# Six small loads of the start, issued by ScalarE instead of GpSimd

## The chip, the cores and the metric

The kernel runs on one core of one Trainium2 chip. The metric is the device time of one execution in microseconds (us); lower is better. Before the change three runs gave 370.06, 370.79 and 371.65 us, a median of 370.79 us.

## What is computed

For 8 batches of 8 heads, 576 tokens and a head dimension of 64, a linear attention is computed with a learned feature map, and then a layer norm and a two-layer feed-forward network with a residual are applied to its result:

```
phi(x) = concat(exp(p - m), exp(-(p - m))),  p = x @ w_phi,  m = max|p| over the 128 features
num = phi(q) @ (phi(k)^T v);  den = phi(q) . sum_s phi(k);  a = num / (den + 1e-6)
x = a with the heads side by side: [8, 576, 512]
out = x + relu(layernorm(x) * g_ln @ w_ch1) @ w_ch2      (512 -> 2048 -> 512)
```

## The kernel before, in words

The work is cut into 32 units of two heads. A unit's 576 tokens make four full tiles of 128 for each head (the main part) and a rest of 64 tokens for each head (the tail). Tails are loaded for four units at a time, one load for each head half: 64 partitions, 4 heads, 64 floats, which is 64 KB in 256 pieces of 256 B. Main parts of the first units are loaded one unit at a time, 256 KB each for q, k and v.

A unit goes through these steps. TensorE transposes k and q (L698 for the main part, L706 for the tail, which needs the tails of both q and k). ScalarE or VectorE copies the result out of PSUM into `qkT` (L715, L713). TensorE multiplies `qkT` with `wbk` (L885 and L900, L813 and L814 for tails). VectorE takes maxima (L953, L817), ScalarE the exponentials (L967, L1033, L830), GpSimd scales v into `vv` (L977 for the main part, L986 for the tail in `vx`). TensorE then forms the products with v (L1059, L1065) and the numerators (L1125, L1133). Eight units make a pair of batches, and the feed-forward of a pair (L1389 for the first layer, L1458 for the second) runs on TensorE between the attention steps of the next.

`wbk` is the bf16 form of `w_phi`, which is needed on partitions 0 to 63 and once more on partitions 64 to 127. So `w_phi` is loaded twice into `wphi_f` (L415 and L416), and VectorE casts the two halves one after the other (L463).

The order on every engine is written ahead of time by a planner (class `Order`). Each step has a rank, a set of engines and an assumed duration; the planner runs through them, gives each a start, and the instructions are emitted in order of these starts. A few operations that come first in the program, the two loads of `w_phi` and the two first q tails (L429) among them, are emitted before the planner runs; the planner only counts time for them. The planner's steps of the start, on the two queues that matter, are these:

```
add("POOL", 1.3, -9.0, None)
add("ACT", 1.3, -9.0, None)
dma("POOL", -8.9, 65536, None, w=[("qx0", 0)], us=0.65, row=4096)
add("POOL", 0.7, -8.8, None)
dma("POOL", -8.7, 65536, None, w=[("qx1", 0)], us=0.65, row=4096)
load_main("q", 0, 1, -4.0, "ACT")
load_tails("v", 0, -3.0, "POOL")
load_main("v", 0, 1, -3.0, "ACT")
add("ACT", 1.3, -1.0,
    lambda: nc.scalar.preload_act_table_set("natural_log_exp_and_others"))
```

A load issued by ScalarE counts 0.53 us in the plan. DMAs issued by SyncE (SP) and ScalarE share eight semaphores, which they take in turn; a ninth DMA can be issued only when the one eight before it has landed. DMAs issued by GpSimd have eight of their own.

Until 75 us of the plan the planner puts small matmuls that nobody reads (L1665, writing `n_bank` from a tile of zeros) into every gap of TensorE, so that it has work. They stand in TensorE's queue like any other instruction and are always executed.

Of the kernel before, what the change touches and what calls it, by code (L numbers as in the profile page):

```python
# [359 lines left out]
def kernel(  # L360
# [13 lines left out]
    nc = tc.nc  # L374
    P = 128

    B, H, S, D = q.shape
# [35 lines left out]

    wphi_f = consts.tile([P, F], FP32, name="wphi_f")
    nc.scalar.dma_start(out=wphi_f[0:D, :], in_=w_phi)  # L415
    nc.gpsimd.dma_start(out=wphi_f[D : 2 * D, :], in_=w_phi)  # L416
    gln_sb = consts.tile([P, KC], FP32, name="gln")
    ngln = consts.tile([P, KC], FP32, name="ngln")

# [1 line left out]
    qx_bufs = [consts.tile([P, TG, 2, D], FP32, name=f"qx{i}") for i in range(2)]  # L421

    def first_q_tail(half):

        src = bass.AP(
            tensor=q.tensor, offset=q.offset + (half * S + 4 * P) * D,
            ap=[[D, 64], [2 * S * D, TG], [1, D]],
        )
        nc.gpsimd.dma_start(out=qx_bufs[0][half * 64 : half * 64 + 64, :, 0, :], in_=src)  # L429

    first_q_tail(0)
    make_identity(nc, ident)
    first_q_tail(1)

    wz = consts.tile([P, P], BF16, name="wz")
# [29 lines left out]
    for i in range(2):  # L465
# [7 lines left out]
        out=nident, in0=ident, scalar1=minus, scalar2=None, op0=ALU.mult  # L473
# [64 lines left out]
    def dma(queue, rank, nbytes, emit, r=(), w=(), us=0.53, tiles=0, row=1024, late=1.7):  # L538


        key = ("dma", len(sched.ops))
        kind = "DMA_w" if queue == "POOL" else "DMA"
        if tiles:
            packets, ns, lag = tiles * 8 + BARRIER / 0.018, 0.018, LAND_T + sched.slack[2]
            us = Turn(1.3)
        elif queue == "POOL":
            packets, ns, lag = nbytes / row / 16, 0.081, LAND_W
            if row == 4096:
                packets, ns, lag = 16 * packets, 0.022, LAND_W + late
        else:  # L550
            packets, ns, lag = nbytes / row / 16, 0.018 if row <= 256 else 0.048, LAND
            lag += sched.slack[1]
            us = 0.66 if row == 256 else us
        ns *= sched.slack[3]
        pieces = max(1, round(packets * ns / 1.2))
        lanes = ("SW", 1) if queue == "POOL" else ("HW", 1)
        add(queue, us, rank, emit, r=r, w=(key, *w), acquire=lanes, load=(kind, packets * ns))
        for i in range(pieces):
            last = i == pieces - 1
            add(kind, Move(packets / pieces, ns), rank, None, r=(key, *r) if last else (key,),  # L560
                w=(*w, key) if last else (key,), lag=lag if last else 0.0,
                release=lanes if last else None)

    def issue(queue, rank, dst, src, keys, nbytes, row=1024, hold=False, n=1):
        eng = {"SP": nc.sync, "ACT": nc.scalar, "POOL": nc.gpsimd}[queue]

        def emit():
            load = eng.dma_start(out=dst, in_=src)
            if hold:
                wait_for_w2(load)  # L570

        dma(
            queue, rank, nbytes, emit, r=[("w2 came", HOLD)] if hold else (), w=keys, row=row,
            us=0.65 if queue == "POOL" else 0.53, late=1.7 + 1.4 * (n == 0),
        )
# [5 lines left out]
    def wait_for_w2(load):  # L581
        tc.add_manual_dep(
            load.ins, w2_loads[HOLD].ins.name,
            mybir.DependencyInfo(mybir.DependencyClass.Sync, mybir.DependencyReason.DATA),
            reason="weights first",
        )

    def load_main(key, n, nu, rank, queue):

        t = {"q": q, "k": k, "v": v}[key]  # L590
        pair, i = divmod(n, H)
        g, u0 = divmod(n, HG)
        buf = v_bufs[g % NBUF] if key == "v" else qk_bufs[g % NBUF][:, "qk".index(key)]
        dst = buf[:, u0 : u0 + nu, :]
        us = range(u0, u0 + nu)
        b, h, _ = heads(pair, i, 0)
        src = bass.AP(
            tensor=t.tensor, offset=t.offset + (b * H + h) * S * D,
            ap=[[4 * D, P], [S * D, 2 * nu], [1, 4 * D]],
        )  # L600
        issue(
            queue, rank, dst.rearrange("p u (a f) -> p (u a) f", a=2), src,
            [(key + str(half), g % NBUF, u) for u in us for half in range(2)]
            + [("came", key, n)],
            262144 * nu, hold=12 <= n < 2 * H,
        )

    def load_tails(key, n, rank, queue):

        t = {"q": q, "k": k, "v": v}[key]  # L610
        pair, i = divmod(n, H)
        j = n // TG % 2
        for half in range(2):
            b, h, step = heads(pair, i, half)
            ps_ = slice(half * 64, half * 64 + 64)
            dst = vx_bufs[j][ps_, :, half, 0:D] if key == "v" else (
                qx_bufs[j][ps_, :, "qk".index(key), :]
            )
            src = bass.AP(
                tensor=t.tensor, offset=t.offset + ((b * H + h) * S + 4 * P) * D,  # L620
                ap=[[D, 64], [step * S * D, TG], [1, D]],
            )
            issue(
                queue, rank, dst, src, [(key + "x" + str(half), j)], 16384 * TG,
                row=4096 if queue == "POOL" else 256, hold=12 <= n < 2 * H, n=n,
            )
# [957 lines left out]
    for n in range(NU + 2):  # L1584
# [48 lines left out]
        if n >= 1 and n <= NU:  # L1633
# [4 lines left out]
            half, i = i % 4 // 2 if i % 2 else None, i % 4 + 4 * (i == 7)  # L1638
# [67 lines left out]
```

## Time and profile before

| what | value |
|---|---|
| three runs | 370.06, 370.79, 371.65 us |
| median | 370.79 us |
| profiled execution, its own time | 369.84 us |
| its span, first to last instruction | 367.8 us |
| TensorE busy | 357.9 us, 97% |
| VectorE, ScalarE, GpSimd busy | 249.9, 266.5, 211.7 us |
| mean granted TensorE clock | 0.999 |

The span is what the trace covers; the execution's own time is 2.04 us longer, for what lies around the span. The profiled execution is 0.95 us below the median of the runs. PE is TensorE, DVE VectorE, ACT ScalarE, POOL GpSimd, SP SyncE; a q behind a name stands for the sequencer that issues. TensorE's busy time holds the matmuls on zeros too.

### The profile page before, as it was taken

To read this page: it belongs to the slowest core of one execution; us is meant where nothing else is said; L and a number is where in the kernel's file an instruction comes from. 1 tells how busy PE (TensorE), PEld (TensorE's weight loads), DVE (VectorE), ACT (ScalarE), POOL (GpSimd) and SP (SyncE) were. 2 spreads that over 40 slices of the span, in tenths; PEclk is the share of its full clock that TensorE was granted. 3 is DMA by queue.
4 is the path that set the end of the run, shared out by engine and by line. 5 is a ranking of instruction groups with operands and counts; after the bars stand their busy time and mean duration, and the time that the engine had idled before them with its cause. 6 is when DMAs were issued, how large, how long until landed. Compare 5 with 4: busy or idle time off the path is not lost.

```text
span 367.8 us, 9571 instructions
## 1 busy us (share of the span) xinstructions
PE 357.9 (97%) x3673; PEld 223.4 (61%) x3673; DVE 249.9 (68%) x572; ACT 266.5 (72%) x583; POOL 211.7 (58%) x368
## 2 busy tenths in 40 slices
PE   8889899999999999999999999999999999999996
PEld 8788765556576555555666645455666665555544
DVE  4677887798889969878989857987797754000001
ACT  3789978669899977794979686957787666444430
POOL 4449537787867397666778775747557263110111
PEclk9999999999999999999999999999999999999999
DMA  7999999979976678579667443671403003400012
GB/s 201 315 221 258 230 246 261 258 181 297 217 130 210 129 212 177 177 110 219 189 189 114 131 91 101 80 178 64 87 6 71 30 31 75 102 29 29 30 57 86
DMA packets 92141, 53.50 MB, mean 145 GB/s; under 512 B 58544, under 2 KB 87536, under 8 KB 92096
## 3 DMA queue, kind: packets, MB, share of 16 engines
q1 hardware_dynamic: 87056, 47.86, 53.6%
q0 software_dynamic: 4416, 4.49, 7.2%
q8 instruction: 28, 0.46, 0.5%
q10 hardware_dynamic: 624, 0.56, 0.5%
q14 instruction: 17, 0.14, 0.1%
HBM read 36.77 MB, written 9.44 MB: 126 GB/s over the span
## 4 chain that ended last, share of the span: by engine, by line
PE 84%; DVE 6%; ACT 5%; DMA 3%; issue 1%; DVEq 0%; ACTq 0%
PE b_bank L1389 31%; PE b_bank L1458 30%; PE n_bank L1665 4%; PE n_bank L1065 4%; PE a_bank L891 3%; DMA qkT<-b 3%; PE a_bank L1133 2%; PE a_bank L900 2%; DVE m L953 2%; PE n_bank L1059 1%; ACT ea L1033 1%; ACT hT_all L1033 1%; PE b_bank L1423 1%; ACT hT_all L967 1%; PE n_bank L1133 1%
## 5 line engine op out<-in xcount | busy, mean ns | idle before, releaser
L1389 PE MATMUL b_bank<-xT,w 128*128 128x384 bf16 (+2 forms) x768 | 148.2, 326 | 0.9 <-ACT hT_all L1400 0.9
L1458 PE MATMUL b_bank<-w,hT_all 128*128 128x512 bf16 x560 | 144.6, 379 | 0.0
L1389 PEld LDWEIGHTS <-w 128*128 128x128 bf16 x768 | 71.2, 98 | 53.5 <-issue 1.9
L1400 ACT ACTIVATE hT_all<-b_bank 128x384 bf16<-128x384 f32 (+2 forms) x123 | 60.3, 491 | 51.1 <-PE b_bank L1389 50.1
L953 DVE TENSOR_REDUCE m<-a_bank 128x8 f32<-128x1024 f32 x64 | 77.1, 1218 | 17.6 <-PE a_bank L891 11.8
L1458 PEld LDWEIGHTS <-hT_all 128*128 128x128 bf16 x560 | 50.3, 98 | 42.6 <-issue 1.3
L967 ACT ACTIVATE eb<-a_bank 128x1024 bf16<-128x1024 f32 x60 | 60.8, 1031 | 7.0 <-DVE m L953 3.5
L1033 ACT ACTIVATE ea<-a_bank 128x1024 bf16<-128x1024 f32 x60 | 60.0, 1036 | 3.2 <-PE a_bank L900 2.9
L977 POOL TENSOR_TENSOR vv<-v,em 128x512 bf16<-128x512 f32 x30 | 31.5, 1049 | 44.8 <-ACT em L958 34.2
L1477 POOL TENSOR_TENSOR o<-o,x 128x512 f32<-128x512 f32 x23 | 26.5, 1154 | 51.6 <-ACT o L1471 46.2
L1398 DVE TENSOR_SCALAR hT_all<-b_bank 128x384 bf16<-128x384 f32 (+2 forms) x69 | 38.5, 560 | 14.3 <-PE b_bank L1389 12.3
L1242 POOL TENSOR_TENSOR x<-numc,rden 128x384 bf16<-128x384 f32 (+1 forms) x56 | 34.2, 617 | 22.6 <-DVE rden L1167 20.3
L977 POOL TENSOR_TENSOR vv<-v,en 128x512 bf16<-128x512 f32 x30 | 31.4, 1045 | 0.2
L1466 DVE SCALAR_TENSOR_TENSOR o<-b_bank,rstd,x 128x512 f32<-128x512 f32 x12 | 8.9, 744 | 29.1 <-PE b_bank L1458 29.1
L1310 DVE BATCH_NORM_STATS2 st<-x 128x6 f32<-128x256 bf16 (+1 forms) x68 | 26.8, 426 | 2.6 <-POOL x L1242 2.3
L1471 ACT ACTIVATE o<-b_bank,rstd 128x512 f32<-128x512 f32 x23 | 15.9, 691 | 17.4 <-PE b_bank L1458 17.2
L1133 PEld LDWEIGHTS <-ea 128*128 128x128 bf16 x448 | 21.6, 97 | 6.8
L1065 PE MATMUL n_bank<-vv,eb 128*128 128x65 bf16 x480 | 25.2, 194 | 0.0
L1665 PE MATMUL n_bank<-wz 128*128 128x120 bf16 x307 | 23.9, 228 | 1.0 <-DVE KV L1073 1.0
L772 POOL TENSOR_TENSOR b<-qk,one 128x1024 bf16<-128x1024 f32 x13 | 24.6, 1892 | 0.5 <-DMA qkT<-b 0.3
L1065 PEld LDWEIGHTS <-eb 128*128 128x128 bf16 x480 | 20.9, 98 | 3.8
L1665 PEld LDWEIGHTS <-wz 128*128 128x128 bf16 x308 | 20.0, 105 | 2.3 <-issue 1.3
(131 smaller groups left out, 502.2 us busy)
## 6 DMA issues: line engine op xcount, KB each, us to landing
out_dram<-o SPq DMA_DIRECT2D x31, 256.0 KB, 2.5
qk<-in_k_dram SPq DMA_DIRECT2D x12, 512.0 KB, 5.8
qk<-in_q_dram SPq DMA_DIRECT2D x12, 512.0 KB, 6.8
v<-in_v_dram SPq DMA_DIRECT2D x12, 512.0 KB, 4.8
w<-in_moe_w_ch_dram POOLq DMA_DIRECT2D x8, 512.0 KB, 11.8
qk<-in_k_dram SPq DMA_DIRECT2D x8, 256.0 KB, 7.3
qk<-in_q_dram SPq DMA_DIRECT2D x7, 256.0 KB, 7.6
v<-in_v_dram SPq DMA_DIRECT2D x7, 256.0 KB, 7.0
```

The source lines that it names most:

```text
L953: nc.vector.reduce_max(out=m, in_=ps, axis=AX.X, apply_absolute_value=True)
L967: nc.scalar.activation(eb, ps, AF.Exp, scale=(1.0, -1.0)[t])
L977: nc.gpsimd.tensor_tensor(out=u["vv"][:, t, 0:MX, 0:D], in0=vb[:, hh, :].rearrange("p (c d) -> p c d", d=D), in1=bcast(e[:, 0:MX], 2, D), ...
L1033: nc.scalar.activation(u["EA"][:, t, 0:1024], u["pt"], AF.Exp, scale=(1.0, -1.0)[t])
L1065: nc.tensor.matmul(ps[:, t, c // 4, :], EB[:, t, c, :], vv[:, t, c, :], start=False, stop=(t == 0 and c == MX - 1), skip_group_check=True,)
L1133: nc.tensor.matmul(ps[t][:, i, :], ea(u, t, c), KV[:, t, c // 4, :], start=True, stop=True,)
L1242: nc.gpsimd.tensor_tensor(out=x_, in0=num, in1=rd, op=ALU.mult)
L1389: nc.tensor.matmul(st["ps"], w1_sb[:, kc, jj * P : (jj + 1) * P], xT_bufs[(pair * NR + r) % XB][:, kc : m * KC : KC, :], start=(kc == 0), ...
L1398: nc.vector.tensor_relu(h_sb, st["ps"])
L1400: nc.scalar.activation(h_sb, st["ps"], AF.Relu)
L1458: nc.tensor.matmul(ch[t], hT[r, jj][:, rt * P : (rt + 1) * P], w2_sb[:, jj, :], start=(jj == 0), stop=(jj == JC - 1),)
L1665: nc.tensor.matmul(banks[res][i][:, 0:WN] if res else warm, wz, wz[:, 0:WN], start=bool(res), stop=bool(res), skip_group_check=True,)
```

## The change

Three lines are touched. The second load of `w_phi` (L416) and the two first q tails (L429) are issued by ScalarE. In `issue`, every queue that is not SP becomes ScalarE; the only caller that names POOL is the first load of the v tails, so the two v tails are issued by ScalarE as well. The load of `g_ln` and those of the feed-forward weights name GpSimd themselves and stay there. The planner still takes all of these to be GpSimd's, so the order that it writes does not change.

```diff
     nc.scalar.dma_start(out=wphi_f[0:D, :], in_=w_phi)
-    nc.gpsimd.dma_start(out=wphi_f[D : 2 * D, :], in_=w_phi)
+    nc.scalar.dma_start(out=wphi_f[D : 2 * D, :], in_=w_phi)
...
-        nc.gpsimd.dma_start(out=qx_bufs[0][half * 64 : half * 64 + 64, :, 0, :], in_=src)
+        nc.scalar.dma_start(out=qx_bufs[0][half * 64 : half * 64 + 64, :, 0, :], in_=src)
...
-        eng = {"SP": nc.sync, "ACT": nc.scalar, "POOL": nc.gpsimd}[queue]
+        eng = nc.sync if queue == "SP" else nc.scalar
```

## Rows read from the trace of the kernel before

**Rows 1.** The page, part 1: engine, busy us, share, instructions.
```profile
PE 357.9 (97%) x3673; PEld 223.4 (61%) x3673; DVE 249.9 (68%) x572; ACT 266.5 (72%) x583; POOL 211.7 (58%) x368
```

**Rows 2.** Stretches: us; busy PE, PEld, DVE, ACT, POOL; granted clock, DMA share, GB/s.
```profile
30.00:40.00 10.00, 8.91 (x191) 7.99 (x188) 8.71 (x29) 9.95 (x22) 9.33 (x19) 1.00 1.09 249
...
90.00:100.00 10.00, 9.14 (x97) 5.71 (x96) 8.40 (x19) 8.06 (x20) 8.36 (x15) 1.00 1.02 175
...
120.00:140.00 20.00, 20.00 (x195) 11.29 (x194) 17.12 (x40) 17.18 (x39) 13.23 (x24) 1.00 0.80 192
```

**Rows 3.** The chain of waits from 0 to 12 us: start, us, what.
```profile
5.18 0.40 PE b_bank L698 x4
...
9.23 0.53 issue
```

**Rows 4.** ScalarE and its queue, 0 to 25 us: start, us, what, idle before.
```profile
0.75 0.55 ACTq L415 DMA_DIRECT2D wphi_f<-in_w_phi_dram  x1
1.33 0.60 ACTq L568 DMA_DIRECT2D qk<-in_q_dram  x1
1.96 0.49 ACTq L568 DMA_DIRECT2D v<-in_v_dram  x1
2.48 1.28 ACT L1575 ACT_TABLE_LOAD   x1 [2.48 <-issue]
5.62 0.59 ACT L715 COPY qkT<-b_bank 128x512 bf16<-128x512 bf16 x1 [1.86 <-PE b_bank L698]
...
7.87 0.58 ACT L715 COPY qkT<-b_bank 128x512 bf16<-128x512 bf16 x1
...
10.18 0.26 ACT L715 COPY qkT<-b_bank 128x128 bf16<-128x128 bf16 x1
```

**Rows 5.** TensorE's matmuls, 5.2 to 10 us, in the same columns.
```profile
6.31 0.60 PE L885 MATMUL a_bank<-wbk,qkT 128*128 128x256 bf16 x4
6.77 0.40 PE L698 MATMUL b_bank<-ident,qk 128*128 128x128 bf16 x4
```

**Rows 6.** GpSimd, 0 to 25 us, in the same columns.
```profile
1.26 0.72 POOL L416 DMA_DIRECT2D wphi_f<-in_w_phi_dram  x1 [0.81 <-POOLq L1690]
...
3.72 1.23 POOL L568 DMA_DIRECT2D vx<-in_v_dram  x2
...
11.73 1.05 POOL L977 TENSOR_TENSOR vv<-v,em 128x512 bf16<-128x512 f32 x1 [6.03 <-ACT em L958]
...
12.87 0.40 POOL L986 TENSOR_TENSOR vv<-vx,em 128x130 bf16<-128x130 f32 x1
```

**Rows 7.** SyncE's queue, 0 to 25 us, in the same columns.
```profile
1.25 1.41 SPq L568 DMA_DIRECT2D qx<-in_k_dram  x2
...
6.74 0.37 SPq L568 DMA_DIRECT2D qk<-in_q_dram  x1
```

**Rows 8.** Whom SyncE's queue waited for, 6.6 to 6.8 us: us, times, longest.
```profile
SPq L568 <- DMA qk<-in_q_dram: 1.7, 1, 1.7
```

**Rows 9.** VectorE's timeline, 0 to 25 us.
```profile
3.73 0.22 DVE L463 CAST wbk<-wphi_f 64x128 bf16<-64x128 f32 x1 [1.34 <-DMA wphi_f<-in_w_phi_dram]
5.69 0.22 DVE L463 CAST wbk<-wphi_f 64x128 bf16<-64x128 f32 x1 [1.75 <-DMA wphi_f<-in_w_phi_dram]
```

**Rows 10.** DMA issues, 0 to 25 us: count, KB each, us from issue to landing.
```profile
qk<-in_q_dram ACTq DMA_DIRECT2D x1, 256.0 KB, 5.4
...
qx<-in_q_dram POOLq DMA_DIRECT2D x2, 64.0 KB, 6.3
vx<-in_v_dram POOLq DMA_DIRECT2D x2, 64.0 KB, 7.3
```

**Rows 11.** Two more stretches, columns as in the second group.
```profile
4.00:12.00 8.00, 7.47 (x116) 6.97 (x115) 4.58 (x11) 3.58 (x7) 1.97 (x4) 1.00 1.09 254
12.00:18.00 6.00, 5.46 (x88) 4.86 (x85) 3.98 (x8) 5.03 (x7) 4.25 (x8) 1.00 1.09 347
```

**Rows 12.** Who waited for whom, 10 to 50 us, all engines: us, times, longest.
```profile
PE b_bank L1125 <- ACT KV L1075: 1.3, 1, 1.3
```

## The prediction

> **What bounds the kernel now.** I began with the busy shares [rows 1]: TensorE is busy for 97% of the span, so what matters is where it stands still or does work that nobody needs. The stretches come next [rows 2]. From 120 us on TensorE is busy for 20.00 of 20 us; there, whatever delays its queue delays the end by as much. From 30 to 40 us it is ScalarE that is full (9.95 of 10 us), while TensorE fills its time with matmuls on zeros. So the first 45 us or so are set by the round of ScalarE, VectorE and TensorE for each unit, the rest mostly by TensorE. The third view is the list of waits from 10 to 50 us [rows 12]. The reader is to see what is not there: no line of it names a DMA, and TensorE's longest wait is 1.3 us for ScalarE. The loads of the first units are therefore ahead of the work, and what starts the round late makes all of it late.
>
> The change lies in the first 12 us, so I read the chain of waits there [rows 3] and then each queue [rows 4 to 7, 9]. The round starts with the transposes of k, which the chain ends at 5.18 + 0.40 = 5.58 us. ScalarE copies them out at 5.62 us, having been idle for 1.86 us until then [rows 4]. Behind that copy stands the product at L885, at 6.31 us [rows 5], then the exponentials, the copies of q and of the tails, up to 10.18 us [rows 4]. The copy at 5.62 us is the place to watch.
>
> **What leaves GpSimd.** Five issues: the second `w_phi` at 0.72 us, two v tails in 1.23 us, and two q tails of the same size as these, 3.2 us in all [rows 6]. GpSimd's first scaling at 11.73 us waits for ScalarE after 6.03 us of nothing, so the time that it gains is worth nothing.
>
> **What comes to ScalarE.** The same five issues, in two places. The second `w_phi` and the q tails stand ahead of the planner's steps, hence right behind the first `w_phi` and ahead of the main loads of q and v. The v tails are emitted where the plan has them: on GpSimd at 1.3 + 0.65 + 0.7 + 0.65 = 3.30 us of the plan, while ScalarE's table load is planned at 1.3 + 2 x 0.53 = 2.36 us and its first copy comes after both. So ScalarE's order is: w_phi, w_phi, q tail, q tail, q, v, table load, v tail, v tail, copy.
>
> Prices: a `w_phi` issue 0.55 us [rows 4]. No tail was issued by ScalarE; the nearest rows are SP's, two in 1.41 us [rows 7], and GpSimd's, two in 1.23 us [rows 6]. I take SP's, a queue of the same kind in the same microseconds. Between two issues lie 0.03 us [rows 4]. From the first start:
>
> 0.75 + 2 x 0.55 (w_phi) + 1.41 (q tails) + 0.60 (q) + 0.49 (v) + 1.28 (table) + 1.41 (v tails) + 8 x 0.03 = 7.28 us.
>
> The first copy moves from 5.62 to 7.28 us, by 1.66 us. With tails at GpSimd's price it is 2 x 0.18 = 0.36 us less.
>
> Two things bound this term. Below: whether ScalarE's queue issues the v tails while the table load runs, no row shows. If it does, the copy starts at 7.28 - 1.28 = 6.00 us, 0.4 us late. I take the serial value, since all that the rows show of this queue is one thing after the other [rows 4]. Above: the eight shared semaphores. SP's eleventh such DMA (q at 6.74 us) was held for 1.7 us until the third, the first q, had landed [rows 7, 8]. With five more of them at the start, ScalarE's q becomes about the ninth and waits for the first `w_phi`, whose landing released a cast at 3.73 us [rows 9]; by the sum it is due at 3.38 us, so that it is held for 0.35 us and ends 0.1 us late if an issue that waited takes 0.37 us, as SP's did [rows 7]. The v tails are about the fourteenth and sixteenth and wait for a k tail and the second k. If the last one draws the main q load instead, issued at about 3.7 us and landing 5.4 us later as before [rows 10], it is held until 9.1 us and the copy starts at about 9.5 us, 3.9 us late. I expect these landings sooner than before, because the packets of GpSimd's queue go: the core moved 254 GB/s while they were there and 347 GB/s behind them [rows 11]. So I add only the 0.1 us for q, less a little for tails between the two prices: 1.7 us.
>
> **What else moves.** The main q load is issued 2.1 to 2.4 us later. Before, it landed at 1.33 + 5.4 = 6.73 us, just in time for the transposes at 6.77 us [rows 4, 5, 10]; with the copy of k and L885 moved by 1.7 us they are due at 8.5 us. Issued at 3.7 us it lands at 9.1 us by its old latency, and at 6.7 us by the 3.0 us of the first `w_phi` (0.75 to 3.73 us) [rows 4, 9]. The first would cost 0.6 us, as TensorE's queue is in order; I take nothing, by the GB/s above, and keep the 0.6 us for the range. The v tails, issued at 6 to 7 us, land by 14.2 us even at 7.3 us each [rows 10], and L986 needs them at 12.87 + 1.7 = 14.6 us [rows 6]. The second `w_phi` comes sooner; its cast at 5.69 us [rows 9] was done at 5.91 us, ahead of the copy's end at 6.21 us, and held nobody.
>
> The q tails come sooner too. TensorE waits for a DMA once in the start: 0.53 us at 9.23 us, ahead of L706, until the second q tail is there [rows 3]. That wait goes, but the copy of the tails runs at 10.18 us straight behind ScalarE's exponentials, with no idle time before it [rows 4], so it buys nothing.
>
> **How far the shift carries.** Behind the copy all waits are for engines [rows 12], so the round moves as a whole; the matmuls on zeros are executed in any case and take nothing up. TensorE's idle time between 90 and 100 us is 10.00 - 9.14 = 0.86 us [rows 2]; at most that could take some of it up. I count nothing. Sum: 369.84 + 1.7 = 371.5 us for the profiled execution, which lay 0.95 us below the median; against the median of the runs 370.79 + 1.7 = 372.5 us, 0.46% more.
>
> **Rivals.**
>
> *The semaphores hold ScalarE.* For it: the 1.7 us that SP was held [rows 8]. Against it: the loads concerned should land sooner. The copy is 2.2 to 3.9 us late: 373.0 to 374.7 us.
>
> *The issues are cheap.* The v tails go out beside the table load and the copy is 0.4 to 1.2 us late: 371.2 to 372.0 us. For it: an issue is the sequencer's work and the table load the engine's. Against it: no row has the two together.
>
> *Not slower: the start is set by the tails' landing.* Place: L706, held for 0.53 us [rows 3], which a sooner landing gives back. It decides if the first copy comes less than 0.53 us later, that is, only with the v tails beside the table load, and if the copy of the tails would have run sooner without that wait. Then 370.79 + 0.4 - 0.53 = 370.7 us; with the 0.86 us near 95 us taken up as well, 369.8 us. Against it: ScalarE has no gap ahead of 10.18 us [rows 4]. The Trainium skill (DMA: Bandwidth & Descriptors, Issuing engine by pattern) has loads issued by SyncE or ScalarE generally faster than GpSimd's, which speaks for this rival: by that rule alone the change would be a gain. The rows bear it out so far that GpSimd's tails took 6.3 and 7.3 us to land [rows 10], but they show no work except L706's waiting for them.
>
> *The change does not move the copy at all* only if the v tails were emitted behind it; the plan's times exclude that.
>
> **How the numbers follow.** Issues in series: 0.50, 372.1 to 372.9 us, likeliest 372.5 us. Semaphores: 0.20. Cheap issues: 0.19. Not slower: 0.11. The range leaves out the upper part of the second (above 374.2 us) and most of the last (below 371.0 us): 371.0 to 374.2 us. About 0.5% (1.85 us, below 368.94 or above 372.64 us) is what a measurement of this kernel can tell from no change. Above that lie two fifths of the first case and all of the second: 0.40. Faster by as much: 0.03, out of the last case, if the loads gain more than I see. Within it: 0.57.
>
> **What would show it.** ScalarE's queue with eight issues, the last ending near 7.2 us; the first copy at 7.3 us; TensorE idle for 1.6 us ahead of the first L885; no wait at L706; GpSimd empty from about 2.5 to 13 us; behind 120 us the same steps as before, 1.7 us later. I am wrong if the copy starts before 6.4 us (the table load hides the tails) or after 7.8 us (a semaphore holds them), if the q load is late for its transposes, or if the shift seen at 20 us is no longer there at 120 us.

## The result, and the profile after

The changed kernel takes 371.53 us (median of 20 runs, 370.34 to 372.75). 20 runs of the kernel before, taken beside them, have a median of 370.25 us (368.96 to 371.65). The ratio is 1.0032, with a 95% interval of 1.0017 to 1.0047: 1.2 to 1.3 us slower, within the 0.5% that the prediction called no change. It had said 372.5 us. Of the 0.97 us between, 0.54 us is the base, since the three runs shown ahead of the prediction lay above the 20 runs (370.79 against 370.25 us). The 1.7 us added to that base met 1.28 us, but not for the reasons that were given, as the rows and the runs below show.

The profiled execution after took 370.43 us, with a span of 368.6 us; before it was 369.84 and 367.8 us. ScalarE's queue from 0 to 13 us is the first view (start, us, what, idle before), and its rows answer to [rows 4]:

```profile
0.74 0.57 ACTq L415 DMA_DIRECT2D wphi_f<-in_w_phi_dram  x1
1.34 0.62 ACTq L416 DMA_DIRECT2D wphi_f<-in_w_phi_dram  x1
1.99 1.37 ACTq L429 DMA_DIRECT2D qx<-in_q_dram  x2
3.85 0.41 ACTq L568 DMA_DIRECT2D qk<-in_q_dram  x1
4.30 0.47 ACTq L568 DMA_DIRECT2D v<-in_v_dram  x1
4.80 1.28 ACT L1575 ACT_TABLE_LOAD   x1 [4.80 <-DMA wphi_f<-in_w_phi_dram]
6.28 1.32 ACTq L568 DMA_DIRECT2D vx<-in_v_dram  x2
7.64 0.58 ACT L715 COPY qkT<-b_bank 128x512 bf16<-128x512 bf16 x1 [1.55 <-DMA qk<-in_k_dram]
8.93 1.02 ACT L967 ACTIVATE eb<-a_bank 128x1024 bf16<-128x1024 f32 x1 [0.70 <-PE a_bank L885]
10.14 0.58 ACT L715 COPY qkT<-b_bank 128x512 bf16<-128x512 bf16 x1 [0.19 <-PE b_bank L698]
```

The order is the forecast one. Two holes stand in it that no issue fills. From 3.36 to 3.85 us the q load is held until the first `w_phi` has landed (3.83 us in the trace). The table load ends at 6.08 us, and the copy at 7.64 us names a DMA as what it waited for: the load of the second unit's k. That load is no input of the copy. It is the DMA whose semaphore the second v tail takes over; that tail stands ahead of the copy in ScalarE's queue, and is issued only when the load has landed. In the trace the second k tail landed at 6.20 us and the first v tail was issued at 6.28 us; the second k load landed at 6.94 us, the second v tail was issued at 6.96 us and the copy began at 7.64 us.

TensorE's matmuls from 8 to 13 us, in the same columns, against [rows 5]:

```profile
8.28 0.61 PE L885 MATMUL a_bank<-wbk,qkT 128*128 128x256 bf16 x4 [2.55 <-ACT qkT L715]
9.71 0.40 PE L698 MATMUL b_bank<-ident,qk 128*128 128x128 bf16 x4 [0.81 <-DMA qk<-in_q_dram]
...
12.00 0.22 PE L706 MATMUL b_bank<-ident,qx 128*128 128x128 bf16 x1
```

It waits twice: 2.55 us for the copy, then 0.81 us for the main q load, issued at 3.85 us. The chain of waits of the first 13 us, against [rows 3], names only the second of these, as it ended last:

```profile
0.74 3.09 DMA wphi_f<-in_w_phi_dram
...
3.85 5.81 DMA qk<-in_q_dram
...
9.71 0.40 PE b_bank L698 x4
```

The wait at L706 is gone, as forecast. Before, its weight load stood for 0.78 us:

```profile
9.73 0.10 PEld L706 LDWEIGHTS <-qx 128*128 128x128 bf16 x1 [0.78 <-issue]
```

Its going takes up a part of q's delay: L885 for q, just ahead of it, is 2.93 us later than before, and L706 itself 2.17 us. On GpSimd the first scaling has moved from 11.73 to 14.19 us, against [rows 6], with 11.55 us of nothing ahead of it:

```profile
14.19 1.05 POOL L977 TENSOR_TENSOR vv<-v,em 128x512 bf16<-128x512 f32 x1 [11.55 <-ACT em L958]
```

How much later is the rest? The order on TensorE is the same in both kernels, so its 3,673 weight loads can be matched one by one ("late" is against the first profile of the kernel before, here and below). The k product (L885) is 2.02 us later than before, the q transposes 2.93 us, and from the tails at 12 us on everything is 2.2 us later (2.16 us between 60 and 95 us). There it falls to 1.14 us within one instruction and stays there to the end: the last operation, on VectorE, starts at 365.34 us after and 364.20 us before. (The span grew by 0.8 us, since the last store landed 0.3 us sooner behind it.) The stretches show where the 1.0 us went, and answer to [rows 2, 11] (us; busy PE, PEld, DVE, ACT, POOL; granted clock, DMA share, GB/s):

```profile
90.00:100.00 10.00, 10.00 (x119) 6.54 (x118) 9.34 (x20) 9.37 (x23) 8.55 (x15) 1.00 1.10 203
...
4.00:12.00 8.00, 4.64 (x76) 4.13 (x74) 2.66 (x8) 4.24 (x5) 0.00 (x0) 1.00 1.05 278
```

TensorE's 0.86 us of idle time between 90 and 100 us is gone. In the kernel before, this is what stood there, on ScalarE and on TensorE:

```profile
94.31 1.04 ACT L770 CAST b<-qk 128x1024 bf16<-128x1024 f32 x1 [1.42 <-DMA qkT<-b]
...
95.79 1.95 PE L1389 MATMUL b_bank<-xT,w 128*128 128x384 bf16 x11 [0.86 <-ACT hT_all L1400]
```

ScalarE was held for a transposing load (L791) that landed at 94.28 us, and TensorE then for ScalarE. After, the same load landed at 94.46 us, 0.18 us later, though it was issued 2.16 us later (86.78 against 84.62 us). The cast and the matmuls behind it wait for nothing:

```profile
94.94 1.04 ACT L770 CAST b<-qk 128x1024 bf16<-128x1024 f32 x1
...
95.97 0.81 PE L1389 MATMUL b_bank<-xT,w 128*128 128x384 bf16 x4
```

Around 61 us, too, SyncE's loads stand where they stood (the same k load is issued at 60.87 us before and 60.95 us after) while TensorE runs 2.16 us late. So in these two profiles the transfers of that part hardly move with the late start, and TensorE, arriving 2.16 us later, finds its data there. Not every profile is like that: among the runs below, the load that landed at 94.28 us here came at 95.35 us with TensorE on time (v tails alone) and at 97.43 us with TensorE 3.22 us late (added activations).

One thing more is not in this profile. The 20 runs of the changed kernel come with a mean granted TensorE clock each: it is 1.000 in five of them (median 370.59 us) and 0.995 in fifteen (median 371.86 us). The profiled one is of the five. For the 20 runs of the kernel before the clock is not on record; over the 89 runs made beside the experiments it was 0.995 in ten (median 372.73 us) and higher in the others (370.20 us).

### The profile page after: what moved, and what is told of

It reads as the page before. It is cut to its first block, busy times and chain, and to the rows that moved or that the text cites. A ratio compares the mean times of both kernels' runs of the same rounds, so it can differ in the third digit from the quotient of the medians.

```text
span 368.6 us, 9527 instructions
## 1 busy us (share of the span) xinstructions
PE 354.4 (96%) x3631; PEld 222.6 (60%) x3673; DVE 250.4 (68%) x572; ACT 266.6 (72%) x583; POOL 208.7 (57%) x363
## 4 chain that ended last, share of the span: by engine, by line
PE 87%; DVE 5%; ACT 3%; DMA 2%; issue 1%; DVEq 0%
PE b_bank L1389 33%; PE b_bank L1458 31%; PE a_bank L891 4%; PE n_bank L1065 4%; PE n_bank L1665 2%; PE a_bank L1133 2%; PE a_bank L900 2%; DMA qk<-in_q_dram 2%; DVE m L953 1%; PE n_bank L1059 1%; ACT hT_all L1033 1%; PE b_bank L1423 1%; PE n_bank L1133 1%; DMA wphi_f<-in_w_phi_dram 1%; ACT hT_all L967 1%
## 5 line engine op out<-in xcount | busy, mean ns | idle before, releaser
L1458 PE MATMUL b_bank<-w,hT_all 128*128 128x512 bf16 x521 | 137.8, 379 | 2.2 <-issue 0.6
```

The lines of the kernel that those rows point to most:

```text
L1458: nc.tensor.matmul(ch[t], hT[r, jj][:, rt * P : (rt + 1) * P], w2_sb[:, jj, :], start=(jj == 0), stop=(jj == JC - 1),)
```

## The experiments

The theory after the result: semaphores hold ScalarE's queue, and so the first copy; the late q load adds a little; part of the delay is given back near 96 us. The rivals: the sum of the issues, as predicted, sets the copy; the late q load sets the loss; any delay of the first copy costs the same.

### One part alone

Each of the three parts by itself, the rest as before.

```diff
-    nc.gpsimd.dma_start(out=wphi_f[D : 2 * D, :], in_=w_phi)
+    nc.scalar.dma_start(out=wphi_f[D : 2 * D, :], in_=w_phi)
```

> Only the second w_phi is issued by ScalarE. Prediction's account (the copy of k on ScalarE sets the start; a late q load costs nothing): ScalarE has its last start issue done near 4.4 us, the copy stays at 5.6 us or comes earlier, time within 0.3 us of the kernel before. Rival (the landing of the main q load sets the start): q is issued near 1.95 instead of 1.33 us and lands 0.6 us later, the transposes of q move from 6.8 to about 7.4 us, and the time grows by 0.3 to 0.6 us.

Measured: ratio 1.0005 [0.9978, 1.0031]. The copy stands at 5.64 us; the q load, issued 0.65 us later, landed at 7.26 us, and TensorE waits for it:

```profile
7.30 0.40 PE L698 MATMUL b_bank<-ident,qk 128*128 128x128 bf16 x4 [0.29 <-DMA qk<-in_q_dram]
```

That is the place that the rival named. But from 12 us on TensorE is 0.10 us late, as the wait at L706 is gone and takes the rest up. One issue ahead of q eats the margin of that load, and little comes of it. (The 0.48 us behind 96 us in the table below come with the gap there, 1.24 us in this profile.)

```diff
-        nc.gpsimd.dma_start(out=qx_bufs[0][half * 64 : half * 64 + 64, :, 0, :], in_=src)
+        nc.scalar.dma_start(out=qx_bufs[0][half * 64 : half * 64 + 64, :, 0, :], in_=src)
```

> Only the two first q tails are issued by ScalarE. Prediction's account: v waits for the semaphore of the first w_phi until 3.8 us, the table load ends near 5.6 us, the copy of k is less than 0.2 us late, time within 0.3 us. Rival (late main q load): q is issued near 2.75 us, lands at 8.2 to 8.8 us, TensorE waits for it ahead of its transposes for 1.5 us or more with the copy on time, the steps at 20 us are 1 to 2 us late, and the time grows by 0.5 to 1.2 us. A wait of TensorE for a DMA ahead of the transposes of q tells them apart.

Measured: 0.9996 [0.9967, 1.0025]. The copy is on time at 5.70 us, but q, issued at 2.96 us, landed at 8.38 us:

```profile
8.43 0.40 PE L698 MATMUL b_bank<-ident,qk 128*128 128x128 bf16 x4 [1.48 <-DMA qk<-in_q_dram]
```

The q transposes are 1.66 us late; the missing wait at L706 takes 0.77 us of it up, so that TensorE is 0.90 us late from the tails on, until 95.8 us, and 0.12 us early behind it. So a late q load does delay, and in this profile the 0.9 us is given back whole. The rival's 0.5 to 1.2 us of time did not show.

```diff
-        eng = {"SP": nc.sync, "ACT": nc.scalar, "POOL": nc.gpsimd}[queue]
+        eng = nc.sync if queue == "SP" else nc.scalar
```

> Only the two v tails are issued by ScalarE. If the sum of issue times sets the copy: table load until 3.8 us, two issues of 0.7 us, done at 5.2 us, copy on time at 5.6 us, time within 0.3 us. Rival (semaphores): the second v tail draws the semaphore of the main q load, is held until that lands near 6.7 us, the copy comes at about 7.3 us (1.7 us late) although ScalarE issues only five loads, the steps at 20 us are 1 to 1.7 us late, and the time grows by 0.5 to 1.2 us.

Measured: 0.9983 [0.9953, 1.0012]. The v tails were held too, but for loads that landed early (the first `w_phi` at 3.98 us, the main q at 5.01 us), so that the copy did not suffer. The rival had the semaphores right; it counted with q landing near 6.7 us, as before, and in this profile q was 1.7 us sooner:

```profile
4.06 1.57 ACTq L568 DMA_DIRECT2D vx<-in_v_dram  x2
5.67 0.58 ACT L715 COPY qkT<-b_bank 128x512 bf16<-128x512 bf16 x1 [1.89 <-PE b_bank L698]
```

The q tails, still GpSimd's, landed sooner, and L706 came 0.79 us earlier without its wait. L813 behind it, held for the copy of the tails, was 0.02 us later than before: with the copies and q on time, the wait at L706 buys nothing when it goes. Near 96 us TensorE then stood for 1.90 us, and was 1.07 us late behind it, with nothing late at the start.

None of the three parts moves the time by what could be measured, and the three together do. With 12 runs each, the intervals are too wide to say more: that of the second `w_phi` reaches up to 1.0031.

### A copy that is late for another reason

Work is added: four activations of 128x1024 on zeros behind the table load, into a buffer that is free then.

```diff
+    def table():
+        nc.scalar.preload_act_table_set("natural_log_exp_and_others")
+        for _ in range(4):
+            nc.scalar.activation(spare, bcast(wz, 1, 8), AF.Copy)
```

> All loads as before; ScalarE runs four activations of 1024 columns on zeros between the table load and the copy of k (work added, result unchanged), so that the copy comes at 8.0 to 8.7 us, 2.4 to 3.1 us late, with all loads early. If a late start carries in full, as the prediction counted, the time grows by 2.4 to 3.1 us (0.65 to 0.85%). If part is taken up at the transposed load near 95 us, the shift of TensorE's steps is 2.4 to 3.1 us at 20 us and 1.0 us less behind 96 us, and the time grows by 1.4 to 2.1 us. If the missing wait at L706 also gives something back, the shift at 12 us is already smaller than the copy's.

Measured: 1.0044 [1.0020, 1.0069]. The copy is at 8.01 us, 2.39 us late, and TensorE stands still for it (first fence). Then the granted clock falls to its lower level (second fence, stretches with the columns as above):

```profile
8.63 0.61 PE L885 MATMUL a_bank<-wbk,qkT 128*128 128x256 bf16 x4 [1.90 <-ACT qkT L715]
```

```profile
7.00:9.00 2.00, 0.37 (x4) 0.34 (x5) 0.00 (x0) 1.55 (x3) 0.00 (x0) 1.00 1.11 290
9.00:11.00 2.00, 2.00 (x25) 1.99 (x23) 0.66 (x1) 1.50 (x2) 0.00 (x0) 0.59 1.14 258
11.00:13.00 2.00, 2.00 (x21) 1.84 (x19) 0.56 (x1) 1.02 (x1) 0.00 (x0) 0.55 1.09 334
13.00:15.00 2.00, 2.00 (x39) 1.99 (x37) 1.74 (x4) 0.48 (x3) 0.00 (x0) 1.00 1.09 348
```

Before the fall TensorE had stood still for most of 7 to 9 us; the lower level, 0.5 in the trace, is 1.2 GHz, and 25 and 21 matmuls fill stretches where 39 stand behind them. The steps went from 2.4 to 3.2 us late in it. Here nothing was given back: the transposing load landed at 97.43 us in this profile, and TensorE stood for 0.79 us behind it. The median grew by 1.50 us, which is what the expectation gave for a start delay that is partly given back; but the profiled run is the slowest of the twelve (373.27 us), and in it nothing was. What the others did near 96 us is not known. Nine of the twelve runs had a mean clock of 0.995. So a copy late by about as much for another reason costs about what the change costs, as the third rival has it; the intervals allow no closer answer.

### Which of issues and semaphores sets the copy

The table load first, so that it no longer stands between the issues and the copy:

```diff
+    nc.scalar.preload_act_table_set("natural_log_exp_and_others")
     nc.scalar.dma_start(out=wphi_f[0:D, :], in_=w_phi)
     nc.scalar.dma_start(out=wphi_f[D : 2 * D, :], in_=w_phi)
...
-        lambda: nc.scalar.preload_act_table_set("natural_log_exp_and_others"),
+        None,
```

> The changed kernel with the activation table loaded ahead of ScalarE's first issue instead of behind the main v load. If the sum of issue times and table load sets the copy of k and the queue issues loads while the table is loaded, the copy comes at about 6.3 us instead of 7.6 us; if the queue waits for the table, all issues start 1.3 us later and the copy comes at 7.6 us or later. Semaphore theory: the v tails are held until the second k tail and the second k load have landed (6.2 and 6.9 us in the changed kernel), so that the copy stays near 7.6 us even if the first issue starts at 0.75 us. Time like the changed kernel's under the semaphore theory, 0.6 to 1.2 us less under the first.

Measured: 1.0102 [1.0082, 1.0122]. The queue shows both answers:

```profile
0.74 1.28 ACT L415 ACT_TABLE_LOAD   x1 [0.74 <-PEq L1691]
0.78 0.57 ACTq L416 DMA_DIRECT2D wphi_f<-in_w_phi_dram  x1
...
5.00 0.41 ACTq L569 DMA_DIRECT2D qk<-in_q_dram  x1
...
6.14 1.40 ACTq L569 DMA_DIRECT2D vx<-in_v_dram  x2
7.59 0.58 ACT L716 COPY qkT<-b_bank 128x512 bf16<-128x512 bf16 x1 [5.57 <-DMA qx<-in_q_dram]
```

Issues do go out beside the table load: it starts at 0.74 us, the first issue at 0.78 us. Yet the copy, with 1.28 us less in front of it, comes at 7.59 us instead of 7.64. The sum of the issues does not set it; the landings do. Here it was another one: the second v tail had drawn the semaphore of the second q tail, which landed at 6.92 us. The time was missed: it should have been the changed kernel's. The q load had drawn another semaphore, was held until 4.98 us and landed at 10.95 us, so that TensorE waited for it, and its clock was at the lower level by then (the second row is a stretch, columns as above):

```profile
11.00 0.61 PE L699 MATMUL b_bank<-ident,qk 128*128 128x128 bf16 x4 [2.16 <-DMA qk<-in_q_dram]
11.00:13.00 2.00, 2.00 (x21) 2.00 (x21) 0.16 (x1) 1.36 (x2) 0.00 (x0) 0.50 1.08 250
```

So the 5.80 us that TensorE is late in this run hold the cost of the clock as well.

### The q tails behind q and v

```diff
+    def table():
+        first_q_tail(0)
+        first_q_tail(1)
+        nc.scalar.preload_act_table_set("natural_log_exp_and_others")
```

> The changed kernel with the two q tails issued behind the main loads of q and v instead of ahead of them. Theory (two delays, the held copy and the late q): TensorE's wait of 0.8 us ahead of the transposes of q is gone, the copy of k stays at 7.4 to 7.7 us, steps at 12 to 90 us are 1.9 to 2.1 us late against 2.15 us, time 0 to 0.3 us below the changed kernel's. Rival (the q load alone made the loss, as in the run with the q tails alone): steps at 12 us less than 1.3 us late and the time within 0.3 us of the kernel before.

Measured: 1.0100 [1.0076, 1.0123]. The q load is on time (issued 2.00 us, landed 7.27 us), but my expectation for the copy was missed by 2 us, and with it the time:

```profile
8.13 1.54 ACTq L566 DMA_DIRECT2D vx<-in_v_dram  x2
9.71 0.59 ACT L713 COPY qkT<-b_bank 128x512 bf16<-128x512 bf16 x1 [3.18 <-DMA qk<-in_k_dram]
```

(The code is two lines shorter up to there, so L713 is the copy.) With q and v ahead of them, the k tails and the second k load landed later (8.05 and 9.05 us), and the v tails, and so the copy, waited for these. Here, too, the clock was at the lower level behind the wait (0.50 from 11 to 13 us). In the change, in its second profile and here the copy follows the landing of the second k load by 0.70, 0.67 and 0.66 us, which is the issue of one tail and its gap.

### An earlier start, and two second profiles

`FIRST` is the count of leading matmuls on zeros, shortened here beside the move of the second `w_phi`.

```diff
-COLD, FIRST = 5.6, 28
+COLD, FIRST = 5.6, 20
```

> The second w_phi alone on ScalarE, and 20 instead of 28 matmuls on zeros at the start (those are left out), a version meant to be faster. If the start is set by TensorE's leading matmuls and then by the copy: transposes of k at 4.1 to 4.3 us instead of 5.0 us, copy at 4.7 us, steps at 12 us 0.5 to 0.9 us early, time 0.3 to 0.9 us below the kernel before. Rival (the main q load, landing near 7.3 us, and the cast of the second w_phi set it): TensorE waits ahead of L885 or of the transposes of q by as much as it gained, and the time is the same within 0.3 us.

Measured: 1.0025 [0.9999, 1.0051]. The copy came at 4.64 us, a whole microsecond sooner, and TensorE then waited 1.51 us for q, which landed at 7.71 us:

```profile
7.75 0.40 PE L698 MATMUL b_bank<-ident,qk 128*128 128x128 bf16 x4 [1.51 <-DMA qk<-in_q_dram]
```

The rival is right about the wait, and the version is no faster: the q load is right behind the copy as a bound of this start.

> The changed kernel as it is, for a second profile. If the time given back near 96 us belongs to the change, TensorE's steps are 2.0 to 2.3 us late at 20 us and 0.8 to 1.4 us late behind 97 us, and TensorE again has no gap there. If it was one execution's luck, the gap of about 1 us is there and the steps stay 2 us late to the end.

Measured: 371.02 us, span 368.8 us. The copy waits for the second k load as before, with q landing at 8.74 us and no wait for it:

```profile
7.95 0.59 ACT L715 COPY qkT<-b_bank 128x512 bf16<-128x512 bf16 x1 [1.89 <-DMA qk<-in_k_dram]
```

TensorE is 2.3 us late until 95.8 us and 1.28 us behind it. So 1.0 us is given back in both profiles of the change.

> The kernel before once more, for a second profile. Theory (the gap of about 0.95 us in TensorE's first feed-forward steps near 95.8 us belongs to the kernel, since the loads that it waits for are bound by the DMA engines): a gap of 0.8 to 1.4 us there again. Rival (the gap is chance from run to run): none, or under 0.4 us. First copy at 5.6 to 5.7 us by both.

Measured: 369.91 us, span 367.9 us. The gap in TensorE is there again, a little longer:

```profile
95.87 1.95 PE L1389 MATMUL b_bank<-xT,w 128*128 128x384 bf16 x11 [1.14 <-ACT hT_all L1400]
```

It belongs to the kernel before.

### Two parts of three

By now the theory was that the held v tails make the loss. Left on GpSimd, they should give most of it back. The edit is that of the first two parts above, without the third.

```diff
+    nc.scalar.dma_start(out=wphi_f[D : 2 * D, :], in_=w_phi)
...
+        nc.scalar.dma_start(out=qx_bufs[0][half * 64 : half * 64 + 64, :, 0, :], in_=src)
```

> The second w_phi and the two q tails on ScalarE, the v tails left on GpSimd. Theory (the v tails, held in ScalarE's queue until the second k load has landed, make the loss of the whole change): the first copy comes at 5.6 to 6.2 us, as in the runs with one part; the main q load, issued at about 3.5 us, lands at 9 to 9.5 us and TensorE waits 1.5 to 2.5 us for it, steps of 12 us are 1 to 2 us late, and about 1 us of that is given back near 96 us: span +0 to +0.8 us, ratio 1.000 to 1.002. Rival (the late main q load makes the loss, the held copy only hides it): TensorE's steps at 12 us are as late as with the whole change, +2.2 us, and the ratio is 1.003 or more.

Measured: 1.0074 [1.0039, 1.0109], slower by its median than the whole change, though the intervals overlap. The copy is nearly on time, and the rival is right:

```profile
6.07 0.59 ACT L715 COPY qkT<-b_bank 128x512 bf16<-128x512 bf16 x1
```

```profile
10.45 0.40 PE L698 MATMUL b_bank<-ident,qk 128*128 128x128 bf16 x4 [3.13 <-DMA qk<-in_q_dram]
```

The q load was issued at 3.73 us and took 6.7 us; GpSimd's v tails (issued at 1.94 and 2.73 us) were ahead of it now. That these made it slower is not shown: where q is issued at 2.00 us, it took 5.28 us with them (the last version below) and 5.27 us without them (the q tails behind q and v). The q transposes are 3.68 us late, and with 0.77 us taken up at L706 TensorE is 2.95 us late, 1.93 us behind 96 us. Three runs at a mean clock of 1.000 took 371.37, 371.37 and 372.17 us; the six at 0.990 to 0.995 have a median of 374.19 us.

The first and third part, without the second:

```diff
+    nc.scalar.dma_start(out=wphi_f[D : 2 * D, :], in_=w_phi)
...
+        eng = nc.sync if queue == "SP" else nc.scalar
```

> The second w_phi and the v tails on ScalarE, the q tails left on GpSimd. Theory (it takes all three parts to bring the copy behind a held issue): the v tails draw semaphores one or two places earlier than with the whole change, whose loads have landed by 5.0 to 5.5 us, so that the copy starts at 5.6 to 6.0 us; q is issued at 1.9 us and lands at 7.0 to 7.5 us, a wait of 0.3 to 0.6 us; steps at 12 us +0.1 to +0.6 us; ratio 0.999 to 1.002. Rival (v tails behind a second w_phi are enough): the copy comes at 7 us or later and the ratio is 1.003 or more.

Measured: 1.0011 [0.9989, 1.0034]. Here, too, the rival was right about the copy, if not about the ratio: one more `w_phi` ahead of them is enough for the second v tail to draw the semaphore of the first k tail, which landed at 6.89 us. (The row names VectorE as the releaser of the copy; that had ended by 7.11 us, and the tail, issued from 6.91 to 7.57 us, stands in front.)

```profile
4.06 3.51 ACTq L568 DMA_DIRECT2D vx<-in_v_dram  x2
7.62 0.58 ACT L715 COPY qkT<-b_bank 128x512 bf16<-128x512 bf16 x1 [3.18 <-DVE nident L472]
```

TensorE is 2.02 us late, 1.42 us behind 96 us. So there are two delays, and each is enough by itself: a first copy held behind the v tails, and a q load that comes late behind the q tails. They do not add up: with the whole change TensorE is 2.2 us late, with one of them 2.02 or 2.95 us. A late copy of k makes the rest late in full, a late q load by 0.77 us less, and the later of the two counts. In the change they meet almost at the same place (2.02 us, and 2.93 - 0.77 = 2.16 us).

### Both delays taken away

The second `w_phi` and the q tails on ScalarE, with the q tails behind q and v as above; the v tails on GpSimd.

```diff
-    nc.gpsimd.dma_start(out=wphi_f[D : 2 * D, :], in_=w_phi)
+    nc.scalar.dma_start(out=wphi_f[D : 2 * D, :], in_=w_phi)
...
+    def table():
+        first_q_tail(0)
+        first_q_tail(1)
+        nc.scalar.preload_act_table_set("natural_log_exp_and_others")
```

> The second w_phi and the q tails on ScalarE, but the q tails behind the main loads of q and v; the v tails left on GpSimd. Theory (the change has two delays of which the later one counts: a first copy held behind v tails, and a main q load that comes late behind the q tails; each alone is enough): with both taken away, q is issued at 2.0 us and lands at 7.0 to 7.6 us, the first copy comes at 6.3 to 6.8 us, behind two q tails and the table load, TensorE waits less than 0.3 us for q, its steps at 12 us are 0.8 to 1.6 us late (q tails landing at 10 to 11 us may hold L706), 0.9 to 1.0 us of it is given back near 96 us, and the ratio is 0.999 to 1.002. Rival (any longer queue at the start costs what the change costs): steps at 12 us 2 us late or more, ratio 1.003 or more.

Measured: 1.0003 [0.9985, 1.0021], with a mean clock of 0.998 or more in all twelve runs. The copy comes straight behind the table load, with no v tail ahead of it; only the q tails were held, for the two `w_phi` (issued at 3.82 and 4.76 us). The q transposes need no wait. The tails' transposes (L704 here, as this code too is two lines shorter) are held for a q tail that landed at 11.38 us:

```profile
6.70 0.59 ACT L713 COPY qkT<-b_bank 128x512 bf16<-128x512 bf16 x1
```

```profile
7.79 0.39 PE L696 MATMUL b_bank<-ident,qk 128*128 128x128 bf16 x4
...
11.47 0.22 PE L704 MATMUL b_bank<-ident,qx 128*128 128x128 bf16 x1 [1.23 <-DMA qx<-in_q_dram]
```

TensorE is 1.67 us late, and 0.65 us behind 96 us. The expectation held, with the lateness just above the 0.8 to 1.6 us that it gave. No version was measurably faster than the kernel before.

All of them side by side; lateness is TensorE's, as the median over matched weight loads from 60 to 95 us and from 97 to 110 us, in the one profile of each. In the rows of the table load first, of the change with the q tails behind q and v, and of the added activations the lateness holds the cost of the lower clock too:

| kernel | first copy, us | main q landed, us | late, 60 to 95 us | late, 97 to 110 us | ratio | runs with mean clock 0.995 or less |
|---|---|---|---|---|---|---|
| before | 5.62 | 6.73 | 0 | 0 | 1 | 10 of 89 |
| the change | 7.64 | 9.66 | 2.16 | 1.14 | 1.0032 | 15 of 20 |
| the change, second profile | 7.95 | 8.74 | 2.31 | 1.28 | | |
| w_phi | 5.64 | 7.26 | 0.10 | 0.48 | 1.0005 | 0 of 12 |
| q tails | 5.70 | 8.38 | 0.90 | -0.12 | 0.9996 | 2 of 12 |
| v tails | 5.67 | 5.01 | 0.02 | 1.07 | 0.9983 | 1 of 12 |
| w_phi, shorter start | 4.64 | 7.71 | 0.23 | 0.08 | 1.0025 | 4 of 12 |
| w_phi, v tails | 7.62 | 7.16 | 2.02 | 1.42 | 1.0011 | 2 of 12 |
| w_phi, q tails | 6.07 | 10.41 | 2.95 | 1.93 | 1.0074 | 6 of 9 |
| w_phi, q tails behind q and v | 6.70 | 7.28 | 1.67 | 0.65 | 1.0003 | 0 of 12 |
| the change, table load first | 7.59 | 10.95 | 5.80 | 4.78 | 1.0102 | 6 of 6 |
| the change, q tails behind q and v | 9.71 | 7.27 | 4.90 | 3.88 | 1.0100 | 6 of 6 |
| before, added activations | 8.01 | 6.35 | 3.22 | 3.15 | 1.0044 | 9 of 12 |

## Why the prediction was right, and where its steps were not

*ScalarE's order and the price of an issue: right.* Eight issues stand where the plan's times put them. `w_phi` took 0.57 and 0.62 us (0.55 forecast), the q tails 1.37 us (1.41), the v tails 1.32 us (1.41).

*"All that the rows show of this queue is one thing after the other": the serial value was wrong, without effect.* Issues go out beside the table load, as the run with the table load first shows, but the v tails were held past its end anyway.

*"So I add only the 0.1 us for q": this step failed.* The prediction had placed the holds rightly: q behind the first `w_phi` (forecast 0.35 us, it was 0.47 us from the end of the issue before), the v tails behind the second k tail and the second k. It then let them go, since those loads should land sooner. They did land sooner (the second k at 6.94 us, 9.39 us before), only not soon enough. The 347 GB/s that it argued from were not reached: without GpSimd's packets the core moved 278 GB/s from 4 to 12 us, after 254 before. So the copy came at 7.64 us and not at 7.28, and with 1.28 us less in front it still came at 7.59. The size was nearly right because the landing lies close to where the sum ends. It was the first rival's mechanism, at 2.02 us, just below the 2.2 us that the rival began with.

*"I take nothing" for the late q load: failed.* By its old latency, landing at 9.1 us, the prediction had 0.6 us; it was issued at 3.85 us and landed 5.81 us later, and TensorE waited 0.81 us. In the second profile it landed in 4.95 us and nothing waited. Beside the held copy it costs little, as L706 takes up 0.77 us of it; without the held copy it makes TensorE 2.95 us late by itself (w_phi and q tails).

*The wait at L706 buys nothing: right for the copies, not for a late q load.* With the v tails alone it goes, and L813 is 0.02 us later: there is nothing to gain from it, and so the rival that ended at 369.8 to 370.7 us falls. But where q is late, the wait that is gone makes room for it: 0.76 to 0.77 us in the change, the q tails alone, and w_phi with the q tails. The prediction had the wait and the late q load side by side and did not set one against the other. The Trainium skill (DMA: Bandwidth & Descriptors, Issuing engine by pattern) has loads from ScalarE generally faster than those from GpSimd. At first sight the q tails agree: 3.9 us from issue to landing in the change, 6.3 us before [rows 10]. The other runs do not bear it out: issued by GpSimd beside the moved `w_phi` and v tails, the q tails took 4.2 us, and the v tails took 7.1 us from ScalarE in the change and 3.5 us from GpSimd with w_phi and the q tails moved (in this order below). When a load is issued, and beside what, differs between these runs as well, so the engine's share is not shown.

```profile
qx<-in_q_dram ACTq DMA_DIRECT2D x2, 64.0 KB, 3.9
...
qx<-in_q_dram POOLq DMA_DIRECT2D x2, 64.0 KB, 4.2
...
vx<-in_v_dram ACTq DMA_DIRECT2D x2, 64.0 KB, 7.1
...
vx<-in_v_dram POOLq DMA_DIRECT2D x2, 64.0 KB, 3.5
```

The tails came sooner, and nothing that matters was waiting for them, while TensorE was waiting for the main q load behind them.

*"At most that could take some of it up. I count nothing": failed.* Of 2.16 us, 1.02 us is given back at 96 us (1.03 us in the second profile), and 1.02 us also in five of the seven experiments whose TensorE was 0.9 us or more late there; 0.6 us in one and 0.07 us in one. The gap of 0.86 us stood in [rows 2]; that it waits for a transfer could have been read off the trace. That the transfer would come no later could not. By the prediction's own signs it was wrong here (the shift at 20 us is no longer there at 120 us) and in the q load, and the second profile's copy, at 7.95 us, is past its 7.8 us.

*GpSimd's time is worth nothing: right.* Its first scaling waits for ScalarE after 11.55 us of nothing.

*What the prediction did not have: the granted clock.* At a mean clock of 1.000 the change costs 370.59 - 370.25 = 0.3 us by its five such runs, 0.6 us by the first two profiled executions and 1.1 us by the second two (371.02 against 369.91 us); what is left of the 1.28 us comes with the fifteen runs at 0.995. With so few runs the split is rough. In the added activations, the table load first and the q tails behind q and v, the profile shows the lower level directly behind TensorE's standstill. For the change itself it is only argued: TensorE stands still for 2.55 and 0.81 us in the same place, but both its profiles are of runs without the fall, and no profile of a run with it was had. The table speaks for it. TensorE's longest standstill of the start was 1.90 us with the added activations, 2.16 us with the table load first, 2.55 us in the change, 3.13 us with w_phi and the q tails, and 4.59 us with the q tails behind q and v; these are the five kernels with the lower clock in most of their runs (42 of 53). In the others, the kernel before among them, it was 0.29 to 1.51 us, and they had it in 19 of 161. One profile of each stands here beside counts of other runs, so this is support and no proof. A standstill is not always followed by a fall, though: the profile of w_phi and the q tails has none. Also open is why nothing was given back with the added activations, and how far the later give-back varies by itself: with the v tails alone the gap near 96 us grew by 1.0 us in a profile that was on time until then.

So that the forecast came out is in good part luck. Two errors nearly cancel: too little delay at the start (1.7 against 2.16 us) and too little given back (0 against 1.02 us); and a cost of the clock that it did not have lies on top.

## What to carry to other kernels

A DMA issued by a compute engine stands in that engine's order, and if it has to wait for a semaphore, everything behind it waits for a transfer that has nothing to do with it; count the place of each DMA among those that share semaphores and ask when the one eight before it lands, before adding up issue times. Issue first what is needed first: with the small tails put ahead of it, the main q load landed 1.7 to 3.7 us later, and the wait that the tails took away was 0.78 us. Before calling a wait worthless, ask what else it could make room for. A late start need not be carried whole: look for the places where TensorE waits for transfers, and look at the granted clock of all runs, since the profiled one can be of the minority.

## What the runs showed of the hardware

DMA issues of ScalarE's queue run beside its table load (0.74 us for 1.28 us, with an issue at 0.78 us for 0.57 us). The main q load of 256 KB took from 3.66 us (the v tails alone on ScalarE, 1.35 to 5.01 us) to 6.7 us (GpSimd's v tails and ScalarE's q tails issued ahead of it, 3.73 to 10.41 us) to land; two profiles of the change differ by 0.9 us in it (5.81 and 4.95 us), and what part the loads around it have is open. In the profile with the added activations the granted clock fell to its lower level, 1.2 GHz, behind a standstill of TensorE of 1.90 us (0.59 from 9 to 11 us, 0.55 from 11 to 13 us).
